# Attention by head pairs with transposed outputs, decay folded into V, denominators by column-tiled matmuls, and a hand-set TensorE order, in a fused attention and MLP kernel

## The chip, the cores and the metric

The kernel runs on one core of a Trainium2 chip. The metric is device time in microseconds (us), the median over runs. PE is TensorE, PEld its weight loads, DVE is VectorE, ACT is ScalarE, POOL is GpSimd, and SP is the engine that issues most DMAs. An engine name with a q (SPq) is that engine's instruction queue. Runs of one kernel agree within about 1%.

## The reference

The reference computes causal attention with a forget gate for 64 heads (8 batches of 8), followed by an MLP with a SiLU on the 4608 resulting tokens.

```python
# q, k, v: (8, 8, 576, 64); f: (8, 8, 576); w_in: (512, 2048); w_out: (2048, 512)
scores = scale * q @ k.T                       # per head, 576 x 576
cum    = cumsum(log(clip(f, 1e-4, 1)))
scores = where(causal, -1e9, scores + cum[:, None] - cum[None, :])
attn   = exp(scores - max);  attn /= attn.sum(-1) + 1e-9
x      = (attn @ v) reordered to (4608, 512)
h      = x @ w_in
out    = (h * sigmoid(h)) @ w_out
```

The term `cum[:, None]` of a query row cancels in the softmax, so a kernel only needs the factor exp(-cum) of each key.

## The kernel before

Each head is prepared alone. Query and key are cast to bfloat16 side by side, transposed together on PE, and one of the two halves is moved to the other 64 partitions by a DMA (shT), so that the two heads of a pair can use the upper and lower 64 rows of the array at once.

```python
# stage_prep(bh, upper), cut
for c in range(NB):
    nc.tensor.transpose(tp[:, c * P : c * P + n], qk_bf[:n, c, :], ident_bf[:n, :n])
nc.vector.tensor_copy(out=qkT[:, :], in_=tp[:, :])
nc.sync.dma_start(out=sh[0:D, :], in_=qkT[D : 2 * D, :])          # or the other way round
# stage_scores, cut: one exp per head and key block, the decay as its bias
nc.scalar.activation(out=us[i][...], in_=sc[:nk, i, 0:ncols], func=ACT.Exp,
                     bias=negcumT[:nk, kb, bh : bh + 1], scale=scale)
apply_mask(us[i], nk, nk, uoff[kb])                               # DVE copy_predicated
# stage_av, cut: tokens on the partitions, a 65th column of ones gives the denominator
nc.tensor.matmul(av[:nq, qb, :], lhsT=u[:nk, loff : loff + nq],
                 rhs=v_bf[:nk, kb, 0 : D + 1], start=(kb == 0), stop=(kb == qb))
nc.vector.reciprocal(out=rec[:, 0:nfull], in_=av[:, 0:nfull, D])
nc.vector.tensor_tensor(out=y[...], in0=av[...], in1=rec[..., None].to_broadcast(...), op=ALU.mult)
# ... then stage_xT transposes y on PE to get xT, which the MLP needs
```

The MLP is cut into chunks that are queued between the attention work: `hp` (four matmuls of 512 columns, tanh on ACT, one DVE instruction) and `po` (16 matmuls, one ACT copy, one store). A scheduler decides the order on every engine.

The softmax here doesn't subtract the row's maximum and nothing guards it: scores larger than these inputs give would overflow.

## Time and profile before

| | before |
|---|---|
| time | 520.3 us (3 runs, 519.0 to 522.7) |
| PE busy | 448.6 us, 86% |
| mean granted TensorE clock | 0.939 |
| first score matmul, first MLP matmul | 48.2 us, 84.5 us |
| share of the DMA engines' time of the main hardware queue | 27.5% |

The costliest groups: line, engine, operation, output and inputs, shapes, count, busy time and mean ns, then the engine's idle time before them.

```profile
L363 PE MATMUL hp<-xT,w_in_bf 128*128 128x512 bf16 x576 | 148.7, 404 | 0.7
...
L298 PE MATMUL av<-v_bf,uT 128*128 128x65 bf16 (+2 forms) x960 | 86.1, 209 | 11.7 <-DVE uT L234 10.4
```

The two MLP groups (`po`, not shown, is like `hp`) have 576 matmuls each. What one costs at its best is read from the end of the kernel, where nothing else runs. The next lines are the stretches view for 50 us with attention and for 50 us without; the first figure of each pair is busy us, the second (x) the number of instructions.

```profile
core 0: us, PE busy (x) PEld busy (x) DVE busy (x) ACT busy (x) POOL busy (x), PEclk, DMA share, GB/s
250.00:300.00 50.00, 48.31 (x347) 23.69 (x346) 32.24 (x114) 28.51 (x67) 13.26 (x52) 0.93 0.37 93
450.00:500.00 50.00, 50.00 (x233) 22.69 (x232) 19.95 (x29) 21.04 (x36) 3.80 (x7) 1.00 0.09 33
```

Without attention, 233 matmuls in 50 us are 215 ns each. With attention, PE is nearly as busy (48.31 us) but its clock is 0.93.

### The profile page before, as it was taken

To read this page: it belongs to the slowest core of one execution; us is meant where nothing else is said; L and a number is where in the kernel's file an instruction comes from. 1 tells how busy PE (TensorE), PEld (TensorE's weight loads), DVE (VectorE), ACT (ScalarE), POOL (GpSimd) and SP (SyncE) were. 2 spreads that over 40 slices of the span, in tenths; PEclk is the share of its full clock that TensorE was granted. 3 is DMA by queue.
4 is the path that set the end of the run, shared out by engine and by line. 5 is a ranking of instruction groups with operands and counts; after the bars stand their busy time and mean duration, and the time that the engine had idled before them with its cause. 6 is when DMAs were issued, how large, how long until landed. Compare 5 with 4: busy or idle time off the path is not lost.

```text
span 521.1 us, 8830 instructions
## 1 busy us (share of the span) xinstructions
PE 448.6 (86%) x2981; PEld 218.2 (42%) x2981; DVE 290.0 (56%) x954; ACT 257.0 (49%) x572; POOL 107.0 (21%) x433
## 2 busy tenths in 40 slices
PE   0111999978999899999999999999999998999995
PEld 0000544444445444544454445444444444444442
DVE  1103676986783679356844785469447843634400
ACT  1001765656572658255835583557446744434411
POOL 3007223142133213321323132301110100000011
PEclk9999999995899899978998899879998998899999
DMA  8999464447354515351525052501110011001021
GB/s 173 206 205 169 106 148 103 109 112 180 71 129 121 132 38 118 100 137 24 134 71 152 21 126 73 147 23 38 53 53 7 18 53 42 0 26 56 21 81 60
DMA packets 124764, 47.38 MB, mean 91 GB/s; under 512 B 115696, under 2 KB 121840, under 8 KB 124720
## 3 DMA queue, kind: packets, MB, share of 16 engines
q1 hardware_dynamic: 112912, 31.62, 27.5%
q0 software_dynamic: 5472, 13.63, 9.3%
q10 hardware_dynamic: 6336, 1.57, 1.5%
q8 instruction: 23, 0.38, 0.3%
q14 instruction: 21, 0.17, 0.1%
HBM read 36.85 MB, written 9.44 MB: 89 GB/s over the span
## 4 chain that ended last, share of the span: by engine, by line
PE 54%; issue 18%; ACT 10%; DMA 9%; DVE 4%; POOL 3%; SPq 1%; POOLq 0%; ACTq 0%
PE hp L363 18%; PE po L395 13%; PE av L298 11%; ACT uT L273 8%; PE sc L256 7%; DMA qt<-in_q_dram 5%; PE tpqk L212 3%; DMA shT<-qkT 2%; DVE gtile L374 2%; ACT th L371 2%; POOL out_dram L406 2%; DMA qkf<-in_k_dram 1%; PE tpx L338 1%; DMA vt<-in_v_dram 1%; DVE uT L234 1%
## 5 line engine op out<-in xcount | busy, mean ns | idle before, releaser
L273 ACT ACTIVATE uT<-sc,negcumT 128x448 bf16<-128x448 f32 (+4 forms) x384 | 152.3, 489 | 33.0 <-PE sc L256 32.4
L363 PE MATMUL hp<-xT,w_in_bf 128*128 128x512 bf16 x576 | 148.7, 404 | 0.7
L395 PE MATMUL po<-w_out_bf,gtile 128*128 128x512 bf16 x576 | 128.6, 379 | 0.0
L374 DVE SCALAR_TENSOR_TENSOR gtile<-th,hp 128x512 bf16<-128x512 bf16 x144 | 98.5, 685 | 47.4 <-ACT th L371 46.4
L371 ACT ACTIVATE th<-hp 128x512 bf16<-128x512 f32 x144 | 86.6, 601 | 70.4 <-PE hp L363 66.7
L298 PE MATMUL av<-v_bf,uT 128*128 128x65 bf16 (+2 forms) x960 | 86.1, 209 | 11.7 <-DVE uT L234 10.4
L234 DVE COPY_PREDICATED uT<-mask_lo,zeros 128x128 bf16<-128x128 int16 (+1 forms) x320 | 78.4, 275 | 16.2 <-ACT uT L273 12.9
L363 PEld LDWEIGHTS <-w_in_bf 128*128 128x128 bf16 x576 | 55.8, 103 | 71.2 <-issue 20.4
L395 PEld LDWEIGHTS <-gtile 128*128 128x128 bf16 x576 | 55.5, 98 | 64.7
L298 PEld LDWEIGHTS <-uT 128*128 128x128 bf16 (+2 forms) x960 | 57.2, 107 | 48.4 <-DVE uT L234 24.8
L403 ACT ACTIVATE osb<-po 128x512 f32<-128x512 f32 x36 | 21.5, 598 | 108.4 <-PE po L395 82.6
L216 DVE COPY qkT<-tpqk 128x576 bf16<-128x576 bf16 x64 | 28.7, 451 | 64.9 <-PE tpqk L212 63.7
L256 PE MATMUL sc<-qkT,shT 64*128 64x448 bf16 (+1 forms) x192 | 56.0, 318 | 7.1 <-ACT uT L273 3.2
L201 POOL CAST v_bf<-vf 128x256 bf16<-128x256 f32 x64 | 25.5, 399 | 174.3 <-PE av L298 134.0
L212 PE MATMUL tpqk<-ident_bf,qk_bf 128*128 128x128 bf16 (+1 forms) x320 | 36.1, 229 | 28.4 <-DVE qk_bf L197 15.0
L256 PE MATMUL sc<-shT,qkT 64*128 64x448 bf16 (+1 forms) x192 | 56.9, 323 | 2.2 <-DMA shT<-qkT 2.2
L406 POOL DMA_DIRECT2D out_dram<-osb x36 | 19.6, 544 | 160.8 <-ACT osb L403 157.9
L212 PEld LDWEIGHTS <-qk_bf 128*128 128x128 bf16 (+1 forms) x320 | 22.0, 101 | 42.3 <-DVE qk_bf L197 15.2
L197 DVE CAST qk_bf<-qkf 128x512 bf16<-128x512 f32 x64 | 27.0, 422 | 22.6 <-DMA qkf<-in_k_dram 22.2
L256 PEld LDWEIGHTS <-shT 64*128 64x128 bf16 x192 | 16.0, 98 | 27.8 <-issue 20.0
L189 POOL COPY qkf<-qt 64x64 f32<-64x64 f32 x64 | 19.5, 305 | 35.0 <-DVE qk_bf L198 30.0
L313 DVE TENSOR_TENSOR y<-av,rec 128x256 bf16<-128x256 f32 x64 | 25.7, 404 | 0.5
(33 smaller groups left out, 182.1 us busy)
## 6 DMA issues: line engine op xcount, KB each, us to landing
out_dram<-osb POOLq DMA_DIRECT2D x36, 256.0 KB, 2.3
qkf<-in_q_dram SPq DMA_DIRECT2D x61, 128.0 KB, 2.8
qkf<-in_k_dram SPq DMA_DIRECT2D x61, 128.0 KB, 2.9
vf<-in_v_dram SPq DMA_DIRECT2D x61, 128.0 KB, 2.6
shT<-qkT SPq DMA_DIRECT2D x64, 72.0 KB, 2.1
w_in_bf<-in_moe_w_in_dram POOLq DMA_DIRECT2D x1, 2048.0 KB, 18.0
w_out_bf<-in_moe_w_out_dram POOLq DMA_DIRECT2D x1, 2048.0 KB, 32.0
qt<-in_q_dram SPq DMA_DIRECT2D x7, 128.0 KB, 3.2
```

Source lines behind the costliest of these rows:

```text
L197: nc.vector.tensor_copy(out=qk_bf[:, 0 : NB - 1, :], in_=qkf[:, 0 : NB - 1, :])
L212: nc.tensor.transpose(tp[:, c * P : c * P + n], qk_bf[:n, c, :], ident_bf[:n, :n])
L216: nc.vector.tensor_copy(out=qkT[:, :], in_=tp[:, :])
L234: nc.vector.copy_predicated(out=u[:nk, col_off : col_off + nq0], mask=mask_lo[:nk, :nq0], data=zeros[:nk, :nq0],)
L256: nc.tensor.matmul(sc[:nk, i, 0:ncols], lhsT=kT[:, q0 : q0 + nk], rhs=qT[:, q0 + col : q0 + col + ncols], start=True, stop=(not (first and ...
L273: nc.scalar.activation(out=us[i][:nk, uoff[kb] + col : uoff[kb] + col + ncols], in_=sc[:nk, i, 0:ncols], func=ACT.Exp, bias=negcumT[:nk, k ...
L298: nc.tensor.matmul(av[:nq, qb, :], lhsT=u[:nk, loff : loff + nq], rhs=v_bf[:nk, kb, 0 : D + 1], start=(kb == 0), stop=(kb == qb),)
L363: nc.tensor.matmul(hp[:, :ntg], lhsT=w_in_bf[:, cc, fc * P : (fc + 1) * P], rhs=xT[:, cc, t0 : t0 + ntg], start=(cc == 0), stop=(cc == NCC ...
L371: nc.scalar.activation(out=th[:, :ntg], in_=hp[:, :ntg], func=ACT.Tanh, scale=0.5)
L374: nc.vector.scalar_tensor_tensor(out=gte[:, fc, :ntg], in0=th[:, :ntg], scalar=1.0, in1=hp[:, :ntg], op0=ALU.add, op1=ALU.mult,)
L395: nc.tensor.matmul(po[:ntb, :DM], lhsT=gte[:, fc, tb * P : tb * P + ntb], rhs=w_out_bf[:, fc, :], start=(fc == 0), stop=(fc == NFC - 1),)
L406: nc.gpsimd.dma_start(out=out[t0 + tb * P : t0 + tb * P + ntb, :], in_=osb[:ntb, :])
```

## The change

The intent is to give PE less attention work and to lay out its results so that nothing has to be transposed back:

- Two heads are loaded, cast (by POOL now) and transposed together, so the halves come out on the right partitions and the shT DMA disappears.
- The factor exp(-cum) is multiplied into V (by POOL) and kept as a column `w_bf` for the denominators. The exp loses its bias and works on 1024 columns for both heads.
- `num` keeps V as the weights and streams the scores, so its output is already xT: features of two heads on 128 partitions, tokens along the columns. The two heads use two 64-column tiles of the array.
- `den` computes the denominators of four heads at once, in four 32-column tiles. All 32 columns of a tile are the same `w_bf` column, so the 32 output rows of a head are equal.
- One reciprocal takes all four heads. Because xT has features on the partitions, the reciprocals of a head must stand on 64 partitions, and DMAs copy one row of them 64 times.
- Output stores are issued by SP instead of POOL.
- PE's order is set by hand, with MLP chunks as `fill(n)`, and weights are meant to load after the first pairs.

```diff
+    ctx.enter_context(tc.manual_schedule(engines={mybir.EngineType.PE}))
 ... (loads, casts and transposes by pairs: cut)
+        nc.scalar.activation(
+            out=u[:, :, c * 512 : (c + 1) * 512], in_=sc[:, :, :], func=ACT.Exp, scale=scale
+        )
 ... (masks as multiplications: cut)
+    def den(qd):
+        dn = psc.tile([P, 1024], FP32, name="dn", tag="sc")
 ... (loops over key blocks kb, column ranges q0:q1 and the four heads j)
+                    nc.tensor.matmul(
+                        dn[32 * j : 32 * j + 32, q0:q1],
+                        lhsT=w_bf[r, kb, bh : bh + 1].to_broadcast([nk, 32]),
+                        rhs=rhs, ...
+                    )
+        rec = recp.tile([P, S], FP32, name="rec", tag="rec")
+        nc.vector.reciprocal(out=rec[:, :], in_=dn[:, 0:S])
+        for m in range(2):
+            rb = rbp.tile([P, S], FP32, name="rb", tag="rb")
+            for i in range(2):
+                j = 2 * m + i
+                nc.sync.dma_start(
+                    out=rb[i * D : (i + 1) * D, :],
+                    in_=rec[32 * j : 32 * j + 1, None, :].to_broadcast([1, D, S]),
+                )
+            recs[2 * qd + m] = rb
+    def num(n):
 ... (18 matmuls: nm[i*D:(i+1)*D, q0:q1] += vp[:, kb, i, :].T @ u)
+        nc.vector.tensor_tensor(
+            out=xT[:, p, b * S : (b + 1) * S], in0=nm[:, 0:S], in1=rb[:, :], op=ALU.mult
+        )
 ... (MLP chunks: cut; the loop over the 32 pairs n:)
+        scores(n, 0); fill(1); convert(n + 1); load_pair(n + 3); ...
+        scores(n, 1); fill(1); scores(n, 2); fill(2)
+        if n % 2 == 0 and n >= 2:
+            den(n // 2 - 1)
+            fill(2)
+        if n % 2 == 1 and n >= 3:
+            num(n - 3); fill(1); num(n - 2); finished(n - 2); fill(1)
+        if n + 1 < NU:
+            transposes(n + 1)
+        fill(2)
```

The loop is shown with several statements on a line to save space; `dn`, `nm`, `tp` and the scores share two PSUM buffers, and "quad" below means the four heads of one `den`.

## The prediction

> **What bounds the kernel now.** TensorE, after a slow start. The page's busy table gives PE 448.6 us (86%), DVE 56%, ACT 49%; from 150 us on, the windows view shows PE busy 47 to 48 of every 50 us. But it is not at its peak:
> - MLP: 1152 matmuls of 512 columns. In the window 450 to 500 us, with only these left, 233 ran: 215 ns each. All of them need 248 us.
> - Attention: in 150 to 450 us the windows show 739 MLP matmuls (159 us at 215 ns) and 264 score matmuls (22 head pairs). The other 141 us make 6.4 us per pair. It streams only about 1600 (scores, two heads side by side) + 1152 (transposes) + 1950 (av, 65 columns) + 576 columns: 2.2 us at the speed of the MLP matmuls. The rest is weight loads (18 av matmuls took 0.94 us, 52 ns each), waits on the shT DMA and masks, and half clock: the clock records show 0.5 for 3 to 17 us once per batch, mean 0.939.
> - Start: the timeline shows the first scores at 48 us and the first MLP matmul at 84.6 us, behind DMA at 205 GB/s and late q/k tail loads.
>
> **What the change does.**
> - Removed: 960 av matmuls (86 us busy), 160 y transposes (20), 320 masks (78 us DVE), 64 shT DMAs with their waits, exp's bias operand, five small DVE casts and copies per head.
> - Added per pair: 18 column-tiled num matmuls, half of 36 den matmuls. If tiles of one group run together, as the 64-row score pairs do (two 448s both start at 223.55, next 0.20 us later), they stream 1600 + 800 columns. The Trainium skill, "TensorE: Matmul & The Clock Gate", Part 3, states 2.38x for three column tiles; no line of this trace shows column tiles. With weight loads I estimate num 1.1, den 0.6, transposes 1.0, scores 0.8: 3.5 us per pair instead of 6.4.
> - ACT per pair: estimated from the 0.85 ns per element of exp sizes and tanh's 601 ns: three exps of 1024 elements at 1.03 us plus 0.23; total ACT 214 us against 257.
> - DVE: masks about 0.85 us per pair, qkT copy 0.74, xT multiply 0.7. The 576-element reciprocal is dear: 128x4 took 183 ns, 64x1 150, so 8 to 11 ns per element, 5 to 6.5 us, 16 times: 80 to 100 us. DVE total about 250 us.
> - DMA: 64 broadcasts of one row to 64 partitions.
> - Weights load after the first pairs, q/k tails early.
>
> **On the critical path.** First scores at about 15 us; six pairs without MLP filling, bound by DMA (0.8 MB per pair plus weights), ACT 3.3 or DVE 5 us per pair: first MLP matmul about 47 us. Then MLP 248 + 26 pairs x 3.4 = 88 gives 383, plus 5 tail: 388. The reciprocal holds DVE and one of two PSUM buffers, so the next pair's qkT copy and scores come late: 1 to 2 us every second pair, about 15 us more. Predicted 402 us, range 370 to 448. Chances: faster 0.94, same 0.03, slower 0.03.
>
> **What would show it.** First MLP matmul at 40 to 55 us; reciprocals of 5 us or more; num and den groups about 1.1 us per pair and per quad; clock near 1.0 after the start; MLP mean spacing still 215 ns; PE waits before scores, released by the qkT copy, after each den; DVE about 60%.
>
> **What would make it wrong.** Column tiles running one after another (+25 to 40 us). The 64-fold reads of one partition making the broadcast slow: then the xT multiply waits on DMA, blocks DVE and PE every second pair, and the time could pass 450. The opposite: a cheap reciprocal and overlapped weight loads give 370.

## More of the kernel before

The kernels with one run only (E2, E3, E5, E6) have state "unknown", and only differences far larger than 1% are read from them.

The page of the profile, cut. The first lines give busy time and share per engine. Below, each digit is one of 40 slices of the span, in tenths. The last line is the DMA queue of SP.

```profile
span 521.1 us, 8830 instructions
...
PE 448.6 (86%) x2981; PEld 218.2 (42%) x2981; DVE 290.0 (56%) x954; ACT 257.0 (49%) x572; POOL 107.0 (21%) x433
...
PE   0111999978999899999999999999999998999995
...
PEclk9999999995899899978998899879998998899999
DMA  8999464447354515351525052501110011001021
...
q1 hardware_dynamic: 112912, 31.62, 27.5%
```

PE is the busiest engine, nearly full from the fifth slice on, and empty before it. The clock row shows one slice at half speed.

The chain of waits, followed back from the last instruction, by engine:

```profile
PE 54%; issue 18%; ACT 10%; DMA 9%; DVE 4%; POOL 3%; SPq 1%; POOLq 0%; ACTq 0%
```

The DMA issues that matter later (KB each, median us from issue to landing):

```profile
qkf<-in_q_dram SPq DMA_DIRECT2D x61, 128.0 KB, 2.8
...
shT<-qkT SPq DMA_DIRECT2D x64, 72.0 KB, 2.1
```

## The result, and the profile after

The change made the kernel slower: 659.3 us (4 runs, 657.2 to 661.5) against 520.8 us, a ratio of 1.266 (95% interval 1.261 to 1.270). A ratio here and below is the mean time of one kernel's runs over that of the other's of the same rounds, so it is not quite the ratio of the medians.

The page after, the same lines as before:

```profile
span 658.4 us, 7686 instructions
...
PE 428.6 (65%) x3013; PEld 184.5 (28%) x3013; DVE 230.1 (35%) x325; ACT 203.2 (31%) x312; POOL 99.0 (15%) x150
...
PE   3250428767385928775676838592877658907997
...
PEclk9999999979597978878795959687887969957999
DMA  8998787789867774868577674858382825592002
...
q1 hardware_dynamic: 124560, 47.35, 63.0%
```

PE has less to do (428.6 us busy) and DVE too (230.1 us), but PE's share of the span has fallen to 65%. The row of PE swings between full and a third, and the clock falls with it, to 0.864 on average. The SP queue's DMAs now take 63.0% of the engines' time, and moved 47.35 MB instead of 31.62. The bytes alone do not say why: 9.4 MB of the increase are the output stores, which before were in POOL's queue.

The groups: DVE was idle 233.6 us before the multiplies that write xT, waiting for the broadcast, and PE 114.2 us before the MLP group `hp`, waiting for those multiplies.

```profile
L362 PE MATMUL hp<-xT,w_in_bf 128*128 128x512 bf16 x576 | 155.5, 408 | 114.2 <-DVE xT L344 114.2
...
L344 DVE TENSOR_TENSOR xT<-nm,rb 128x576 bf16<-128x576 f32 x32 | 24.2, 758 | 233.6 <-DMA rb<-rec 233.6
...
L311 DVE RECIPROCAL rec<-dn 128x576 f32<-128x576 f32 x16 | 60.1, 3754 | 5.9 <-PE dn L303 5.9
```

The two lines of DMA issues that answer to those of before:

```profile
rb<-rec SPq DMA_DIRECT2D x64, 144.0 KB, 14.1
...
qf<-in_q_dram SPq DMA_DIRECT2D x64, 128.0 KB, 3.0
```

A broadcast of 144 KB from SBUF to SBUF lands after 14.1 us; a load of 128 KB from HBM takes 3.0. The chain of waits, by engine and by line (the second line is cut off by the page); its largest share was PE with 54% before and is DMA with 42% now:

```profile
DMA 42%; PE 20%; SPq 11%; DVE 11%; issue 10%; ACT 5%; POOL 0%; DVEq 0%; ACTq 0%; POOLq 0%
DMA rb<-rec 39%; SPq L316 8%; PE po L389 8%; PE hp L362 8%; DVE rec L311 6%; ACT u L258 4%; SPq L71 2%; DMA kf<-in_k_dram 2%; DVE gt L371 1%; PE sc L251 1%; PE tp L211 1%; DVE xT L344 1%; DVE qkT L220 1%; DMA vf<-in_v_dram 1%; ACT th L370 1
```

What DVE and PE did around one pair of multiplies (start, duration, what, and in brackets the idle time and its releaser), first DVE, then PE:

```profile
229.15 0.18 DVE L278 TENSOR_TENSOR ut<-ut,mask_t 128x64 bf16<-128x64 bf16 x1
236.67 0.76 DVE L344 TENSOR_TENSOR xT<-nm,rb 128x576 bf16<-128x576 f32 x1 [7.34 <-DMA rb<-rec]
245.07 0.76 DVE L344 TENSOR_TENSOR xT<-nm,rb 128x576 bf16<-128x576 f32 x1 [7.65 <-DMA rb<-rec]
247.14 0.69 DVE L371 SCALAR_TENSOR_TENSOR gt<-th,hp 128x512 bf16<-128x512 bf16 x1 [1.31 <-ACT th L370]
```

```profile
231.19 0.86 PE L332 MATMUL nm<-u,vp 128*64 128x512 bf16 x16
...
232.12 0.60 PE L362 MATMUL hp<-xT,w_in_bf 128*128 128x512 bf16 x2
237.48 0.59 PE L362 MATMUL hp<-xT,w_in_bf 128*128 128x512 bf16 x1 [4.75 <-DVE xT L344]
245.89 0.59 PE L362 MATMUL hp<-xT,w_in_bf 128*128 128x512 bf16 x1 [7.82 <-DVE xT L344]
```

Between 229.3 and 245.1 us the trace shows one multiply on DVE and nothing else: the instructions behind it in DVE's order do not pass it. PE stops with it: the MLP matmuls at hand read the very xT that these multiplies write (a chunk of `hp` contracts over all eight heads, and the last four of them are these two pairs), so after 232.12 us one matmul runs after each multiply, at 237.48 and 245.89. The single packets, counted from the DMA records of the traces (every one of these packets carries one row of 2304 bytes):

```
                                             median ns   sum of all, per engine
f load from HBM, before (64 packets)              93
rec broadcast, after (4096, and 64 of f)        1227     254 us of 658
```

The 256 packets of one quad took 18.8 to 20.7 us from first to last over the 16 quads: 256 x 2304 bytes in that time are 28 to 31 GB/s for all 16 engines together.

### The profile page after: what moved, and what is told of

The parts are those of the page before. It is cut to its first block, busy times and chain, and to the rows that moved or that the text cites. A ratio compares the mean times of both kernels' runs of the same rounds, so it can differ in the third digit from the quotient of the medians.

```text
span 658.4 us, 7686 instructions
## 1 busy us (share of the span) xinstructions
PE 428.6 (65%) x3013; PEld 184.5 (28%) x3013; DVE 230.1 (35%) x325; ACT 203.2 (31%) x312; POOL 99.0 (15%) x150
## 3 DMA queue, kind: packets, MB, share of 16 engines
q1 hardware_dynamic: 124560, 47.35, 63.0%
## 4 chain that ended last, share of the span: by engine, by line
DMA 42%; PE 20%; SPq 11%; DVE 11%; issue 10%; ACT 5%; POOL 0%; DVEq 0%; ACTq 0%; POOLq 0%
DMA rb<-rec 39%; SPq L316 8%; PE po L389 8%; PE hp L362 8%; DVE rec L311 6%; ACT u L258 4%; SPq L71 2%; DMA kf<-in_k_dram 2%; DVE gt L371 1%; PE sc L251 1%; PE tp L211 1%; DVE xT L344 1%; DVE qkT L220 1%; DMA vf<-in_v_dram 1%; ACT th L370 1%
## 5 line engine op out<-in xcount | busy, mean ns | idle before, releaser
L362 PE MATMUL hp<-xT,w_in_bf 128*128 128x512 bf16 x576 | 155.5, 408 | 114.2 <-DVE xT L344 114.2
L389 PE MATMUL po<-w_out_bf,gt 128*128 128x512 bf16 x576 | 155.1, 416 | 0.0
L258 ACT ACTIVATE u<-sc 128x1024 bf16<-128x1024 f32 x96 | 97.4, 1029 | 174.6 <-PE sc L251 142.5
L371 DVE SCALAR_TENSOR_TENSOR gt<-th,hp 128x512 bf16<-128x512 bf16 x144 | 95.9, 682 | 65.6 <-ACT th L370 65.6
L344 DVE TENSOR_TENSOR xT<-nm,rb 128x576 bf16<-128x576 f32 x32 | 24.2, 758 | 233.6 <-DMA rb<-rec 233.6
L251 PE MATMUL sc<-qkT 64*128 64x512 bf16 (+4 forms) x320 | 43.3, 345 | 61.3 <-DVE qkT L220 57.0
L389 PEld LDWEIGHTS <-gt 128*128 128x128 bf16 x576 | 54.0, 104 | 70.2 <-issue 23.2
L311 DVE RECIPROCAL rec<-dn 128x576 f32<-128x576 f32 x16 | 60.1, 3754 | 5.9 <-PE dn L303 5.9
L211 PE MATMUL tp<-ident_bf,qk_bf 128*128 128x128 bf16 x256 | 32.8, 268 | 41.3 <-DVE xT L344 29.6
L195 POOL TENSOR_TENSOR vp<-vf,w_bf 128x512 bf16<-128x512 f32 x32 | 33.6, 1051 | 122.8 <-PE nm L332 92.4
L332 PE MATMUL nm<-u,vp 128*64 128x64 bf16 (+4 forms) x512 | 30.0, 264 | 0.2
## 6 DMA issues: line engine op xcount, KB each, us to landing
rb<-rec SPq DMA_DIRECT2D x64, 144.0 KB, 14.1
```

Source lines behind the costliest of these rows:

```text
L195: nc.gpsimd.tensor_tensor(out=vp[:, :, :, :], in0=vf[:, :, :, :], in1=w_bf[:, 0:NM, bh : bh + 2, None].to_broadcast([P, NM, 2, D]), op=ALU ...
L211: nc.tensor.transpose(tp[:, i, c * P : (c + 1) * P], qk_bf[:, i, c, :], ident_bf[:, :])
L251: nc.tensor.matmul(sc[:, i, col : col + q1 - q0], lhsT=t[r, 1, kb * P : (kb + 1) * P], rhs=t[r, 0, q0:q1], start=True, stop=True,)
L258: nc.scalar.activation(out=u[:, :, c * 512 : (c + 1) * 512], in_=sc[:, :, :], func=ACT.Exp, scale=scale)
L311: nc.vector.reciprocal(out=rec[:, :], in_=dn[:, 0:S])
L332: nc.tensor.matmul(nm[i * D : (i + 1) * D, q0:q1], lhsT=v_t[r, p, :] if kb == NM else vp[:, kb, i, :], rhs=(ut[r, :] if kb == NM else u[:, ...
```

## The experiments

Theory A: all 16 DMA engines read the same partition at once, and its way out of SBUF is one port. The Trainium skill, "SBUF — State Buffer", section "Door 1: The DMA port swizzle", says that DMA bandwidth depends on how many of the 16 ports the partitions reach, and gives 435 GB/s for all and 27.2 GB/s for each port. The 28 to 31 GB/s of one quad are slightly above the figure for one port. Theory B: the volume of the copies, or their place in SP's queue among loads and stores. Theory C: the reciprocal of 3.75 us, which holds DVE and one of two PSUM buffers.

### E1: the same bytes from 32 partitions

The 32 rows of a head in `rec` are equal, so two copies of 32 rows replace 64 reads of one.

```diff
-                nc.sync.dma_start(
-                    out=rb[i * D : (i + 1) * D, :],
-                    in_=rec[32 * j : 32 * j + 1, None, :].to_broadcast([1, D, S]),
-                )
+                for h in range(2):
+                    nc.sync.dma_start(
+                        out=rb[i * D + 32 * h : i * D + 32 * h + 32, :],
+                        in_=rec[32 * j : 32 * j + 32, :],
+                    )
```

> The 32 rows of rec of one head are identical, so the same bytes are read from 32 partitions (two copies of 32 rows) instead of 64 times from one. Theory A (all 16 DMA engines queue at one source partition): packets of 2304 B fall from a median of 1227 ns to 90 to 160 ns, the broadcast lands in 2.5 to 4 us instead of 14, DVE's wait for rb falls from 234 us to under 20, the kernel takes 390 to 425 us. Theory B (the 9.4 MB of SBUF to SBUF copies, or their place in SP's queue): bytes, queue and packet size are as before, so it stays above 600 us. Theory C (the 3.75 us reciprocal that holds DVE and a PSUM buffer is the main loss): stays above 580 us.

Measured: 446.3 us (4 runs, 445.5 to 447.4), a ratio to the kernel before of 0.857 (0.854 to 0.860). From the change as it was, this is 213 us less by one edit. Packets fell to a median of 167 ns and one quad to 4.9 us in the typical case. The page, PE's waits and the DMA line:

```profile
span 445.2 us, 7782 instructions
...
PE 387.0 (87%) x3013; PEld 175.2 (39%) x3013; DVE 229.9 (52%) x325; ACT 202.3 (45%) x312; POOL 99.4 (22%) x150
...
PEclk9999999999999999999999999999999999999999
...
rb<-rec SPq DMA_DIRECT2D x128, 72.0 KB, 2.0
```

```profile
PE sc L251 <- DVE qkT L220: 21.0, 13, 3.9
...
PE tp L211 <- DVE xT L345: 8.8, 1, 8.8
```

Landing is 2.0 us and the mean clock is 1.0. B is out: bytes, packet size and queue are the same, and the number of DMAs has even doubled. The time missed A's range by 21 us, though; what is left is taken up in the section on why the prediction was wrong.

### E2: the broadcasts from ACT's queue

```diff
-                nc.sync.dma_start(      # out and in_ unchanged: one row, 64 times
+                nc.scalar.dma_start(
```

> Only the queue changes: the broadcasts are issued by ACT, so they no longer stand between the loads and stores in SP's queue. Theory A: packets still take 1.1 us or more, landing stays at 10 us or more, the time stays at 600 to 680 us. Theory B (order in SP's queue): landing falls to 3 to 5 us and the time below 450 us.

Measured: 639.3 us (one run). Packets stay at 1222 ns and landing at 12.0 us. So the slow packets do not come from SP's queue. The time is 3% shorter, but that is not what the place in the queue is worth: DVE's wait for rb fell to 79.1 us, while ACT now waits in order for `rec` before it can issue, and PE waits 113.7 us for exps. The two effects were not separated.

### E3: half the bytes

```diff
-        rec = recp.tile([P, S], FP32, name="rec", tag="rec")
+        rec = recp.tile([P, S], BF16, name="rec", tag="rec")
...
-            rb = rbp.tile([P, S], FP32, name="rb", tag="rb")
+            rb = rbp.tile([P, S], BF16, name="rb", tag="rb")
```

> rec and rb in bfloat16: half the bytes from the same single partition, the same number of packets. Theory A with a limit in bytes per second at the source: packets of 1152 B take about 610 ns, landing about 8 us, DVE's wait for rb 234 us falls to 60 to 130, the time to 480 to 560 us. If the cost is one per packet, packets stay at 1.2 us and the time within 3% of 659 us.

Measured: 480.2 us (one run), correct within the test's tolerance. Packets of 1152 bytes took 487 ns, landing 7.3 us, and DVE's wait for rb was 47.8 us:

```profile
rb<-rec SPq DMA_DIRECT2D x64, 72.0 KB, 7.3
```

All three are below what A expected, and far from a cost per packet. The packets of one quad took 8.3 to 9.8 us, 30 to 35 GB/s in all, close to the 28 to 31 of the full rows: the cost goes with bytes. (Why the median packet fell to 40% and not to half was not examined.)

### E4: no broadcast at all

`den` is done per pair with 64-column tiles, so that the denominators stand on all 64 partitions and each pair has its own reciprocal.

```diff
-                        dn[32 * j : 32 * j + 32, q0:q1],
-                        lhsT=w_bf[r, kb, bh : bh + 1].to_broadcast([nk, 32]),
+                        dn[D * i : D * i + D, q0:q1],
+                        lhsT=w_bf[r, kb, bh : bh + 1].to_broadcast([nk, D]),
... (the loop over j becomes one over the two heads i of a pair; no DMA)
+            nc.vector.reciprocal(out=rb[:, :], in_=dn[:, 0:S])
```

> No broadcast DMA: den is done per pair with 64-column weights, so that the denominators come out on all 64 partitions, and each pair has its own reciprocal. PE gets 32 groups of about 1.0 us instead of 16 (+16 us), DVE 32 reciprocals of 3.75 us instead of 16 (+60 us). Theory A: no wait on DMA is left, 400 to 450 us. Theory C (reciprocal): twice the reciprocals, so not faster than 659 us by much, above 600 us.

Measured: 501.7 us (4 runs, 500.2 to 503.4), ratio 0.964 (0.960 to 0.967). It removes the DMA waits and is still 55 us slower than E1. Neither range holds it. Its PE waits say a part of why:

```profile
PE sc L251 <- DVE qkT L220: 35.7, 19, 2.8
PE tp L211 <- DVE rb L312: 24.9, 15, 4.1
```

PE waits 61 us for DVE, 31 more than in E1 (21.0 and 8.8): for the qkT copy that stands behind a reciprocal, and for the PSUM buffer that the reciprocal holds. The other 24 us were not taken apart; the 16 more `den` groups on PE, put at 16 us in the expectation, are among them. C is not the cause of the loss of the change, but here the reciprocal holds up PE where it comes ahead of the next pair's copy. The first 16 cost something too, which E7 measures.

### E5 and E6: partition or port

Both replace a broadcast by four copies of 16 rows. By the formula of the page named under theory A, 16 neighbouring rows lie on 4 ports, and 16 rows taken every second on 8.

```diff
-                    in_=rec[32 * j : 32 * j + 1, None, :].to_broadcast([1, D, S]),
+                    in_=rec[32 * j : 32 * j + 16, :],             # E5, four times, 16 rows of out each
+                    in_=rec[32 * j : 32 * j + 31 : 2, :],         # E6, four times
```

> Each broadcast of 64 rows becomes four copies of 16 rows that lie next to each other (partitions 32j to 32j+15). By the Trainium skill's SBUF page these 16 lie on 4 of the 16 SBUF ports. If the limit is one of the port (about 30 GB/s, from 16 packets of 2304 B in 1227 ns), 16 packets share 4 ports: median 280 to 330 ns. If the limit is one of the partition, 16 partitions serve 16 engines without a queue: 90 to 160 ns, as in e1 (167 ns).

> As e5, but every second row (32j, 32j+2, ... 32j+30), which by the same page lie on 8 ports. Port limit: 140 to 180 ns, half of e5 and the same as e1. Partition limit: the same as e5.

Measured: 497.9 and 493.8 us (one run each). Both medians are 132 ns, so the expectation about medians failed. The distributions differ:

```
packets of 2304 bytes by duration      under 250 ns   250 to 310 ns   above
E5, 16 neighbouring rows                      3137            1003      20
E6, 16 rows, every second                     4145               7       8
```

A quarter of E5's packets take about 286 ns (their median), and practically none of E6's. Each DMA here is one packet per engine and they are issued 0.59 us apart, so it is argued here that only the last of the engines that share a port waits for all the others. If four engines share one port, the last one has 4 x 2304 bytes ahead of it and in it, and 286 ns are 32 GB/s, close to the rate of the single row. A limit of the partition alone would have made E5 and E6 equal. So this agrees with the page's map of partitions to ports, as far as these two choices of rows test it. They cannot tell a port from a group of four neighbouring partitions: no run reads only rows that the map puts on one port but 32 apart. That both kernels are slower than E1 has another reason, as far as the trace shows: 16 DMAs per quad, issued one after another by SP, spread the packets of a quad over 9.7 us or more in both, and DVE waits again (63.7 and 59.2 us).

### E7: the next pair's transposes ahead of den

```diff
+        if n + 1 < NU:
+            transposes(n + 1)
         if n % 2 == 0 and n >= 2:
             den(n // 2 - 1)
 ...
-        if n + 1 < NU:
-            transposes(n + 1)
         fill(2)
```

> e1 with the next pair's transposes moved ahead of den and num, so that DVE's copy to qkT no longer queues behind the 3.75 us reciprocal. In e1 PE waits 21 us in total for that copy before scores. If the reciprocal is on the path this way, most of it goes: 425 to 436 us. If the copy only hides another wait (the PSUM buffer that den holds), the wait moves to another tile and the time stays within 1.5% of 446 us.

Measured: 437.1 us (4 runs, 435.8 to 437.8), ratio 0.839 (0.835 to 0.842), 9 us less than E1. After 80 us, E1's PE waited 11.9 us for the qkT copy, seven times; in E7 this wait is gone and 7.1 us for another DVE instruction have come (7 waits before `hp`). The gain misses the expected range by a microsecond: only 11.9 of E1's 21.0 us of waits for the qkT copy lay after 80 us.

### E8: E1 without the hand-set order

```diff
-    ctx.enter_context(tc.manual_schedule(engines={mybir.EngineType.PE}))
```

> e1 without the hand-set order on TensorE, so that the scheduler orders PE as in before. If the hand-set order is a real part of the gain (no gaps, clock at 1.0), this is slower than e1 by 5% or more, 468 to 520 us; if the gain comes from the smaller attention work alone, within 3% of 446 us.

Measured: 438.9 us (4 runs, 438.7 to 439.1), ratio 0.842 (0.840 to 0.845). The hand-set order gains nothing here; the scheduler's order is 1.7% faster than E1 and equal to E7 within 0.5%. The clock is 1.0 without it as well.

### E9, E10, E11: the start

E9 is E7 with the weights later. E10 is E9 with the broadcasts issued by POOL. E11 is E9 without the hand-set order.

```diff
-        if n == 1:
+        if n == 2:
             load_w_in(0)
-        if n == 2:
             load_w_in(1)
 ...
-        if 4 <= n < 8:
-            load_w_out(n - 4)
+        if 6 <= n < 8:
+            load_w_out(2 * n - 12)
+            load_w_out(2 * n - 11)
```

> e7 with the MLP weights loaded later (w_in at pairs 2 and 3, w_out at pairs 6 and 7), so that they share less of the DMA engines with the first pairs' q, k and v. In e7 the first MLP matmul comes at 70 us, where 47 was predicted. If the start is bound by DMA bytes, it comes at 56 to 64 us and the time is 422 to 431 us. If the start is bound by the order on SP's queue or by the chain of DVE and PE, it stays at 68 us or later and within 1% of 437 us.

> e9 with the broadcasts issued by POOL instead of SP, where the first one waited behind loads from 43.6 to 49.1 us although rec was there. If SP's order costs time at the start, the first MLP matmul comes 3 to 6 us earlier than in e9 and the time falls by as much. If POOL's own waiting for rec delays its casts instead, it is 0 to 20 us slower than e9.

> e9 without the hand-set TensorE order. Without it e1 went from 446 to 439 us, the same as moving the transposes by hand. If the two are the same gain, this is within 1% of e9; if the scheduler's order has a further one, 5 us or more faster.

Measured: E9 435.5 us (434.9 to 436.5), ratio 0.837 (0.835 to 0.840), the first MLP matmul at 70.3 us where E7 had 70.1. The two are the same kernel for this question: the trace shows E9's weight loads issued at the times of E7's (w_in at 7.8 to 17 us, w_out from 18.7 to 36 us). A load into a buffer that is used once waits for nothing, so it seems that the scheduler issues it as early as its engine's order allows, wherever it stands in the program. E9 therefore does not test what it was built for. E10, 442.5 us (440.6 to 443.6), ratio 0.851: the first MLP matmul stays at 70.0 us, so issuing the broadcasts from another queue does not bring it forward. It is 7 us slower than E9; POOL now waits 63.9 us for `rec` and is busy 63.3 us with issuing, and which of the two costs the time was not separated. E11, 434.1 us (433.5 to 437.0), ratio 0.836 (0.832 to 0.839): its first MLP matmul came at 61.9 us, but its interval overlaps that of E9.

### E12: the slow broadcast, started earlier

This run asks how the slow broadcast hurts: by its latency, or by taking the DMA engines. It is the change as it was, with one source row, but `den` of a quad runs about 10 us earlier, and there are four `rb` buffers instead of three (cut below, with the last `den` after the loop, which falls away).

```diff
         if n % 2 == 0 and n >= 2:
-            den(n // 2 - 1)
             fill(2)
-        if n % 2 == 1 and n >= 3:
-            num(n - 3); fill(1); num(n - 2); finished(n - 2); fill(1)
+        if n % 2 == 1:
+            if n >= 3:
+                num(n - 3); fill(1); num(n - 2); finished(n - 2); fill(1)
+            den(n // 2)
```

> The change as it was, one source row, but den of a pair of pairs runs at the end of the odd pair instead of in the middle of the next, so that the broadcast has about 10 us longer before num needs it (four rb buffers instead of three, nothing else). If the broadcast hurts only by its latency (14 us), the wait of DVE for rb falls from 234 us to under 60 and the time below 480 us. If it hurts by taking the DMA engines (4 x 4.9 us = 20 us of all 16 engines for two pairs, beside about 8 us for their loads and 2 us for stores, 30 us x 16 = 480 us plus about 40 us of start), it stays at 500 to 560 us however early den is. Over 620 us neither holds.

Measured: 588.8 us (4 runs, 586.6 to 593.5), ratio 1.133 (1.127 to 1.140). This is 71 us faster than the change, but still slower than the kernel before, and 29 us above the range for the second account. The waits of all engines:

```profile
ACT osb L398 <- DMA out_dram<-osb: 97.2, 7, 18.7
...
DVE xT L344 <- DMA rb<-rec: 71.2, 12, 14.4
...
POOL qk_bf L190 <- DMA qf<-in_q_dram: 69.1, 8, 19.3
```

DVE's wait fell from 234 to 71 us. In its place ACT waits 97 us for stores and POOL 69 us for loads. They stand behind the broadcasts in the same rings: the Trainium skill, "DMA: Bandwidth & Descriptors", section "Queues, rings and completion order", says that each DMA engine consumes descriptors in ring order, and this trace agrees, with stores that were waited for up to 18.7 us. SP's timeline fits as well: behind the four broadcasts issued at 263.0 us, the issue of two stores took 10.04 us. (The stores stand in this ring only since the change; leaving them with POOL was not tried.) So it is both. About 70 us were latency that an earlier start hides. The rest is read as DMA time, which no run isolates: the broadcasts of two quads were issued at 235.4 and 263.0 us, and at about 20 us per quad the engines are taken for 20 of these 27.6 us. The sum that gave 520 us for this kernel is too low by 69 us; which part of it is wrong stays open.

### E13 and E14: the weights really held back

E13 is E7, and before each weight load POOL writes one column of its destination, copied from the decayed V of a later pair, so the load has something to wait for. (The load overwrites the column; the result is correct.) E14 is E13 without the hand-set order.

```diff
-        if n == 1:
-            load_w_in(0)
-        if n == 2:
-            load_w_in(1)
-        if n == 3:
-            load_w_in(2)
-            load_w_in(3)
+        if n in (1, 2):
+            for i in (2 * n - 2, 2 * n - 1):
+                c0 = i * DFF // WQ
+                nc.gpsimd.tensor_copy(out=w_in_bf[:, 0, c0 : c0 + 1], in_=vps[n + 1][:, 0, 0, 0:1])
+                load_w_in(i)
         if 4 <= n < 8:
+            nc.gpsimd.tensor_copy(out=w_out_bf[:, (n - 4) * NFC // WQ, 0:1], in_=vps[n + 1][:, 0, 0, 0:1])
             load_w_out(n - 4)
```

> This is E7 with the weight loads really held back: before each one POOL writes one column of the destination tile, copied from a decayed V (vp) of a later pair, so the load cannot be issued before that V exists. (E9 meant to do this, but its loads were issued at the same times as in E7: 7.8 to 17 us for w_in, 18.7 to 36 us for w_out.) If the bytes of the weights bind the start: the first MLP matmul, 70.1 us in E7, comes at 55 to 64 us and the time is 422 to 431 us. If the start is bound by something else (the order of work on DVE, ACT and PE, or SP issuing the first broadcast 10 us after rec is ready): first MLP matmul at 68 us or later, and the time within 1% of E7's 437.1 us (433 to 441). If the weights now come too late, the first MLP matmul waits for a weight DMA and comes after 72 us.

> E13 without the hand-set TensorE order. In E11 (free order) the first MLP matmul came at 61.9 us, in E9 (same, hand-set) at 70.3 us, for a time only 1.4 us shorter. If the hand-set order is what holds the start: 3 us or more below E13, with the first MLP matmul at 62 us or earlier. If not: within 3 us of E13.

Measured: E13 430.9 us (4 runs, 428.2 to 433.1), ratio 0.826 (0.822 to 0.830); E14 429.0 us (427.8 to 431.8), ratio 0.824 (0.821 to 0.828). Both are in range: E13's time and first matmul fit the bytes of the weights, though its runs reach 2 us beyond, and the gate also moves POOL's issuing (0.8 us per load), which was not separated. E14 is within 3 us of E13, so the hand-set order is not what holds the start. E14's first MLP matmul came earlier still, at 51.1 us, for a difference in time that the overlapping runs do not separate: the first matmul alone is a poor measure of the start. The first MLP matmuls in the timelines of PE, E7 and then E13 (start, duration, count, and the wait before):

```profile
70.11 0.65 PE L363 MATMUL hp<-xT,w_in_bf 128*128 128x512 bf16 x2 [0.33 <-issue]
72.46 2.10 PE L363 MATMUL hp<-xT,w_in_bf 128*128 128x512 bf16 x9 [1.70 <-DVE xT L345]
```

```profile
58.34 0.38 PE L363 MATMUL hp<-xT,w_in_bf 128*128 128x512 bf16 x1 [0.17 <-issue]
...
65.12 3.71 PE L363 MATMUL hp<-xT,w_in_bf 128*128 128x512 bf16 x9 [2.33 <-DVE xT L345]
```

The first matmul came 11.8 us earlier, but it found only the first quad's xT. The first run of nine, which needs the second quad, started at 65.12 instead of 72.46 us, and these 7.3 us are what the 6.3 us of the total agree with. (In E13's profiled run, the slowest of its four, the nine matmuls took 3.71 instead of 2.10 us: the granted clock was 0.56 from 45 to 60 us and 0.77 from 60 to 75 us, and 1.00 in E7.) What held the second quad in E13 is read from the chain of waits:

```profile
20.95 15.26 DMA qtf<-in_q_dram
...
43.71 6.07 DMA qf<-in_q_dram
...
53.86 0.52 SPq L317
...
58.23 6.00 DMA rb<-rec
```

Loads of q that take 15.26 and 6.07 us, and eight broadcasts issued by SP one after another, 0.59 us each. The DMA engines' share is still 1.0 or more from 15 to 75 us. E14 has the lowest median of all, 17.6% below the kernel before; its runs overlap with those of E13.

## Why the prediction was wrong

- **The step that failed.** The prediction says under DMA: "64 broadcasts of one row to 64 partitions", with no duration, and its sum "MLP 248 + 26 pairs x 3.4 = 88 gives 383, plus 5 tail: 388" has no term for it. The term was sized at zero. Measured, one such DMA keeps all 16 engines for 64 x 1227 ns / 16 = 4.9 us, a quad for about 20 us, and the xT multiplies wait 233.6 us. Of the 257 us between 402 and 659, E1 removes 213 by changing only the source rows, and its 446.3 us lie in the range predicted for the change, at the upper end. The mechanism was named among the things that could make it wrong ("The 64-fold reads of one partition making the broadcast slow"), with the right consequence, but the chance of a slower kernel was put at 3%, and the broadcast got no cost. It could have had one: the 27.2 GB/s for each port, in the Trainium skill, "SBUF — State Buffer", section "Door 1: The DMA port swizzle", give, as an estimate, 147456 bytes / 27.2 GB/s = 5.4 us for one broadcast that reads one port, 22 us per quad (18.8 to 20.7 were measured), where two pairs have about 23 us in all in E1.
- **The attention work was sized right.** Predicted per pair: num 1.1, den 0.6, transposes 1.0, scores 0.8, together 3.5 us. In E1's timeline between 228 and 242 us, from start to next start: num 0.94, den 0.91 per quad, transposes 0.92, scores 1.12, together 3.4 us. The column tiles do run side by side, which no trace of before could show: 36 den matmuls of 32 columns in 0.91 us stream 1600 columns four times, and one after another the 6400 columns would need 6400 x 215 ns / 512 = 2.7 us.
- **The DVE and ACT sums were right within 8%.** Predicted 250 and 214 us, measured 230.1 and 203.2. The reciprocal took 3.75 us, not 5 to 6.5.
- **The wait after den was right in size.** In E1 after 80 us, PE waits 1.7 us before scores for the qkT copy, as predicted (1 to 2 us), but seven times, after about every second `den` and not after each. E7 shows it to be worth 9 us with what else moves, where 15 were predicted.
- **The start was too short.** The first MLP matmul was predicted at 47 us. With the slow broadcast it came at 85.4 us, in E1 at 72.6, in E7 at 70.1 and in E13 at 58.3. So 11.8 of E1's 26 us are put down to the weight loads by the first matmul, but only 7.3 by the first run that needs the second quad. The loads do not go out after the first pairs, as the change intends, but at 7.8 to 36 us, in the stretch in which the DMA engines are full (E7's share is 1.23 and 1.16 from 15 to 45 us), and they hold up the loads of q, k and v. In E13 the chain still runs through such loads and through SP, and the last 11 us were not taken apart.
- **MLP matmuls before tiled groups cost more.** Predicted was "MLP mean spacing still 215 ns". In E1's timeline, from the start of an MLP group to the start of the next group, four matmuls take 0.97 us and eight 1.83 us where scores, `num` or `den` follow: 0.11 us more per group than 215 ns each. Where transposes follow, which use the whole array, they take 0.87 and 1.74 us, 0.02 us more. (These are the medians of 108 and 24 groups between 90 and 420 us.) Nine of the eleven groups per two pairs stand before a tiled group; 13 times, they make about 13 us, and 18 us are missing in E1 after its first MLP matmul (372.6 measured, 355 predicted). This is an account by addition, not by an experiment. The trace of before shows the same, so the prediction could have read it there: seven MLP matmuls before scores, at 245.56 us, take 1.62 us instead of 1.51, and one before an `av` that uses the whole array, at 244.18 us, takes 0.22.

```profile
230.76 1.04 PE L363 MATMUL hp<-xT,w_in_bf 128*128 128x512 bf16 x4
231.72 0.86 PE L333 MATMUL nm<-u,vp 128*64 128x512 bf16 x16
...
232.66 1.04 PE L390 MATMUL po<-w_out_bf,gt 128*128 128x512 bf16 x4
233.53 0.39 PE L211 MATMUL tp<-ident_bf,qk_bf 128*128 128x128 bf16 x4
```

(E1. The first figure is the start; 128\*64 is the size of the tile of the array. The first group takes 0.96 us up to the next start, the second 0.87.)

- **The clock.** "Near 1.0 after the start" holds in E1 (0.97 to 1.0 over its runs) and not in the change (0.864). E2 and E12, in which PE also waits long, had 0.852 and 0.872; no run here shows what lowers it.

## What to carry to other kernels

A DMA that read one SBUF partition many times moved 28 to 31 GB/s in all, with 16 engines taking part, and loads and stores behind it waited. Taking the same bytes from 32 partitions was the best cure tried (446 us). Letting the matmul write the values where they are needed also removed the wait, but its 16 further reciprocals and `den` groups left it 55 us slower (E4). Cost every new DMA by the partitions it reads and writes, not only by its bytes, and put the cost into the sum. On an engine whose instructions do not pass each other, as DVE's here, place a wait for a DMA so that work which feeds PE does not stand behind it.

## What the Trainium skill lacked or had wrong

- "SBUF — State Buffer", section "Door 1: The DMA port swizzle": its table has 27.6 GB/s measured from four partitions on one port. It lacks the case of one partition that is read many times: 2304-byte packets at a median of 1227 ns with 16 engines, 28 to 31 GB/s together, against 93 ns for the same packet from HBM. The map of partitions to ports agrees with E5 and E6.
- "DMA: Bandwidth & Descriptors", section "Anatomy of one DMA": its fit of 2.0 us plus bytes / 436 GB/s (for DMAs issued by POOL) would give 2.3 us for 144 KB. From one partition the median landing, with four DMAs issued together, is 14.1 us; from 32 partitions it is 2.0 us (72 KB each). The rules for kernel authors on that page name a broadcast only for the number of engines that it uses, and do not warn of reads from one row.
- "VectorE: DVE Perf Modes", section "First, the fixed hardware budget", says that the reciprocal is iterated with a repeat count of 8, but gives no time. Here 128x576 from PSUM takes 3.75 us, 6.5 ns per element.
- "TensorEngine Tiling (Array Packing)", section "Key Properties", says that changing the tiling mode drains TensorE, without a figure. Here a group of full matmuls takes 0.11 us more where a group with smaller tiles follows, and 0.02 us more where one of whole-array matmuls does. No experiment separates the drain from other causes.
- "TensorE: Matmul & The Clock Gate", Part 3, gives 2.38x for three column tiles and no figure for four. Four tiles of 32 columns, 36 matmuls in 0.91 us, are about 2.9x as fast as an estimated 2.7 us one after another.
